# Another hand-annealed order table for a fused attention and feed-forward kernel

## The chip, the core and the metric

The kernel runs on one core of one Trainium2 chip. A core has a matrix engine (TensorE, PE in the profile), a vector engine (VectorE, DVE), a scalar engine (ScalarE, ACT), a general engine (GpSimd, POOL) and a sync engine (SyncE, SP) that here only issues DMAs. Each engine has a queue of its own that it works through strictly in order, and the engines meet through semaphores. The metric is the device time of one execution in microseconds. The kernel before took 668.05 us, the median of three runs from 667.8 to 668.63.

## What is computed

One transformer layer with 2048 tokens of width 640, attention with 32 query heads of width 20 that share one key head and one value head, and beside it a feed-forward block of width 1536 with a squared ReLU. Both read the same normalised input, and both results are added to the input:

```python
xn = _layernorm(x, axis=-1)
return x + _A_ref(xn, A_wq, A_wk, A_wv, A_wo) + _B_ref(xn, B_w1, B_b1, B_w2, B_b2)
# _A_ref: scores = q k^T * Dh**-0.5; p = softmax(scores); o = p v; out = o wo
# _B_ref: h = relu(x w1 + b1)**2; out = h w2 + b2
```

The scores are 32 x 2048 x 2048 numbers, and each has to go through an exponential.

## The kernel before

**Tiles and stages.** A block is four heads by 512 queries, and there are 32 blocks. Within a block the 2048 keys are cut into 16 key tiles of 128. A score tile is one head, 128 keys and 512 queries: one matmul with 20 rows of contraction into one of the seven free banks of PSUM, and there are 2048 of them. The matmuls of up to four heads sit in four row strips of the matrix engine and run side by side; the text calls such a set of score matmuls a **burst**. Everything else on the matrix engine runs in four column strips of 32: the sums of probabilities times values, the projections, the feed-forward layers and the output. Changing between row strips and column strips is a change of mode.

**Two ways to the exponential.** 696 instructions on ScalarE take two score tiles each (L1274, tile PT). The other 656 tiles make 164 **sets** of four: VectorE turns each tile into 16-bit integers that, read as bf16, are an exponential with a straight line between powers of two (L1497). Three more copies of the set with shifted integers are made by **passes**, either on GpSimd (an INT64_ADD, L1517) or on VectorE (L1518, with both listed at L1517 and L1518 as the alternatives `POOL` and `DVE`). The four copies are terms of one better exponential. They are summed by the matrix engine in that each term is multiplied with the values and accumulated (tiles x_sb or tmore with vx or vxs). Two terms of equal weight can instead be added first: by a DMA with accumulation that GpSimd issues (L1534), called a **pair sum**, or by VectorE (L1539, or L1913 where it was chosen afterwards). Then the matrix engine has one group of four matmuls less. The accumulators of a block are all in one bank.

**Who sets the order.** A greedy planner inside the kernel (L1648 and after) first makes a list of instructions for each engine. Then the table `PLAN` (L414) replaces these lists: for each engine it holds, entry by entry, how far down the list of instructions not yet taken the next one stands. A zero takes the next one. The key `on` has one digit for each of 820 choices (five for each of 164 sets): for three passes whether GpSimd (0) or VectorE (1) makes them, and for two pairs whether the matrix engine takes both terms (0), a DMA adds them (1) or VectorE adds them (2). The key `held` names, for instructions of GpSimd, the instruction of VectorE that they have to wait for, so that the two don't use the shared access to memory at the same time.

**The replay.** The function `replay` (L298) walks the five ordered lists once while the program is built, with a duration for each instruction and a latency for each dependence (the inner function `reach`, L307). On the chip the order on each engine is that of the table. What replay decides is which bank of PSUM a score tile or an accumulation takes (the one that it holds to be free first), the order in which waits are worked out, and which first and last matmul of a block opens and closes the sum. The same rules were used outside the kernel to anneal the table.

Of the kernel before, what the change touches and what calls it, by code (L numbers as in the profile page):

```python
# [79 lines left out]
ADM = 0.7  # L80
ADMP = 0.7
ADLEAD = 1.24
# [89 lines left out]
STOP = None  # L172
# [122 lines left out]
RC = dict(SAME=0.0027, CR=0.105, RC=0.098, FIRST=0.010, LANE=0.004, ACT=0.9035, ACTPE=0.2215, POOLP=1.008, AD=0.915, QK=0.425, DVEPE=0.155, STOP=114, STOPT=1.2)  # L295


def replay(seq, pool, order_all):  # L298
    ptr = {e: 0 for e in seq}
    free = {e: 0.0 for e in seq}  # L300
    start, fin, land = {}, {}, {}
    order_all.clear()
    mode, lock, dma, nadd, lastlock = "C", 0.0, 0.0, 0, None
    lane = [0.0] * HPG
    held = {}

    def reach(d, o):  # L307
        if d.dma is not None:
            return land[d] + ((ADMP if o.eng == "PE" else ADM) if d.add and not o.add else 0.0)
        if o.add and d.eng == "POOL":  # L310
            return fin[d] + ADPL + 0.035
        if d.eng == "PE":
            if o.eng == "PE":
                return start[d]
            return start[d] + (RC["QK"] if d.mode == "R" else d.dur + 0.2005) + (0.0 if o.eng == "ACT" else 0.02)
        if d.eng == "ACT" and o.eng == "PE":
            return fin[d] + (RC["ACTPE"] if d.name[:3] == "ACT" else LATS["ACT", "PE"])
        if d.eng == "DVE" and o.eng == "PE":
            return fin[d] + RC["DVEPE"]
        return fin[d] + LATS.get((d.eng, o.eng), 0.1)  # L320

    while True:
        best = None
        for e, ops in seq.items():
            if ptr[e] >= len(ops):
                continue
            o = ops[ptr[e]]
# [8 lines left out]
            for d in o.deps:  # L336
                t = max(t, reach(d, o))
            if o.lock:
                t = max(t, lock)
                if e == "POOL" and lastlock is not None:  # L340
                    t = max(t, fin[lastlock] + LATS["DVE", "POOL"])
# [32 lines left out]
        if e == "PE":  # L374
            if o.mode == "R":
                held["t"], held["o"] = t, o
                for h in o.lanes:
                    lane[h] = t + 0.2133 + RC["SAME"]
# [1707 lines left out]
```

## Time and profile before

| what | value |
|---|---|
| median of three runs | 668.05 us |
| the profiled execution | 669.29 us |
| its span from first to last instruction | 667.5 us |
| granted clock of the matrix engine | 1.000 |
| ScalarE exponentials (L1274) | 696, 641.1 us busy |
| score matmuls | 2048 |
| DMA pair sums (L1534) | 122 |
| DMA traffic | 100.51 MB |

The profiled execution is 1.24 us longer than the median, and 1.8 us of it lie around the span. The profile is one execution. Its page gives busy times for each engine, groups of instructions with mean duration, and the chain of work that ended last. Matmuls overlap in the pipeline, so a matmul's listed duration is longer than the time from one start to the next, and a busy matrix engine can still be waiting a little. All matmuls of the column strips and of the scores come from one helper, line L675, so they are told apart by tile names: `ps<-qT,kT` is a score matmul.

### The profile page before, as it was taken

The numbers are of one execution on the slowest core, as the hardware profiler recorded it, in microseconds if no ns is written. First come the engines' busy times: TensorE is split into PE (matmuls) and PEld (weight loads), VectorE is DVE, ScalarE is ACT, GpSimd is POOL, SyncE is SP. The second block draws the span as 40 slices with busy tenths as digits, with TensorE's granted clock in tenths as the row PEclk, the third lists the DMA queues.
The fourth block names the chain that finished last, engine by engine and source line by source line (L and its number), as shares of the span: only waits on it lengthen the run. The fifth ranks groups of instructions, "written<-read, shape, count | busy, mean of one in ns | idle before, by whom it ended". The sixth has DMA issues, their size and how long they took to land.

```text
span 667.5 us, 22412 instructions
## 1 busy us (share of the span) xinstructions
PE 659.2 (99%) x9618; PEld 213.7 (32%) x9618; DVE 623.0 (93%) x1120; ACT 650.2 (97%) x719; POOL 538.9 (81%) x549
## 2 busy tenths in 40 slices
PE   8999999999999999999999999999999999999998
PEld 4532222332322223333332222233233322223345
DVE  8879999899899999999999999999999999999997
ACT  7999999999999999999999999999999999999995
POOL 1608899998998898898888999988889999888600
DMA  8893756888768997777868577677688776438642
GB/s 290 233 249 76 149 98 145 162 178 169 144 147 167 182 178 145 153 152 154 165 133 165 112 156 145 134 155 136 145 166 172 138 144 137 96 63 165 142 108 76
DMA packets 53208, 100.51 MB, mean 151 GB/s; under 512 B 15980, under 2 KB 31228, under 8 KB 53044
## 3 DMA queue, kind: packets, MB, share of 16 engines
q0 software_dynamic: 18224, 66.59, 53.7%
q1 hardware_dynamic: 34308, 32.11, 16.8%
q8 instruction: 75, 1.23, 0.8%
q10 hardware_dynamic: 576, 0.38, 0.2%
q14 instruction: 25, 0.20, 0.1%
HBM read 23.26 MB, written 10.01 MB: 50 GB/s over the span
## 4 chain that ended last, share of the span: by engine, by line
PE 89%; DMA 6%; POOL 3%; DVE 1%; issue 0%; ACT 0%
PE ps L675 88%; DMA x_sb<-tmore 3%; POOL tmore L1517 1%; DMA x_sb<-x_sb 1%; DMA tmore<-tmore 1%; POOL x_sb L1517 1%; PE ps L880 1%; PE ps L851 0%; POOL tmore L1534 0%; PE ps L910 0%; PE ps L812 0%; DVE tmore L1497 0%; DVE OR L752 0%; ACT PT L1274 0%; DVE ident L689 0%
## 5 line engine op out<-in xcount | busy, mean ns | idle before, releaser
L1274 ACT ACTIVATE PT<-ps 128x1024 bf16<-128x1024 f32 x696 | 641.1, 1114 | 5.8 <-PE ps L675 5.2
L1497 DVE TENSOR_SCALAR tmore<-ps 128x512 uint16<-128x512 f32 x656 | 424.8, 683 | 25.2 <-PE ps L675 16.3
L675 PE MATMUL ps<-qT,kT 20*128 20x512 bf16 x2048 | 265.0, 384 | 0.5 <-ACT PT L1274 0.5
L1517 POOL INT64_ADD tmore<-tmore x200 | 216.0, 1119 | 36.4 <-DVE big L1008 17.4
L1517 POOL INT64_ADD x_sb<-tmore x202 | 219.7, 1117 | 20.0 <-DVE big L1008 6.2
L675 PEld LDWEIGHTS ps<-qT,kT 20*128 20x128 bf16 x2048 | 68.2, 91 | 253.4 <-issue 75.7
L675 PE MATMUL ps<-PT,vx 128*32 128x512 bf16 x1392 | 130.0, 384 | 0.0
L675 PE MATMUL ps<-w_sb,big 128*32 128x320 bf16 x1536 | 80.0, 302 | 0.0
L675 PE MATMUL ps<-xnT,w_sb 128*32 128x512 bf16 x960 | 77.7, 383 | 0.0
L1534 POOL DMA_DIRECT2D tmore<-tmore x63 | 63.3, 1004 | 9.1 <-DVE tmore L1518 4.7
L675 PE MATMUL ps<-x_sb,vxs 128*32 128x512 bf16 x624 | 59.5, 383 | 1.0 <-DMA x_sb<-x_sb 1.0
L675 PE MATMUL ps<-tmore,vxs 128*32 128x512 bf16 x632 | 60.4, 383 | 0.0
L1534 POOL DMA_DIRECT2D x_sb<-tmore x54 | 52.4, 970 | 5.3 <-POOL x_sb L1517 3.0
L675 PE MATMUL ps<-tmore,vx 128*32 128x512 bf16 x528 | 50.8, 384 | 0.6 <-DMA tmore<-tmore 0.6
L675 PEld LDWEIGHTS ps<-PT,vx 128*32 128x32 bf16 x1392 | 33.5, 94 | 39.5 <-issue 34.0
L675 PEld LDWEIGHTS ps<-w_sb,big 128*32 128x32 bf16 x1536 | 33.1, 95 | 30.6 <-issue 22.0
L1000 DVE TENSOR_SCALAR hT_tmp<-ps,b1col 128x512 bf16<-128x512 f32 x48 | 35.7, 743 | 2.9 <-PE ps L675 2.4
L1518 DVE TENSOR_SCALAR tmore<-tmore 128x2048 uint16<-128x2048 uint16 x47 | 32.8, 708 | 1.4 <-PE ps L675 1.3
L675 PE MATMUL ps<-x_sb,vx 128*32 128x512 bf16 x328 | 32.0, 384 | 1.1 <-DMA x_sb<-tmore 1.1
L675 PE MATMUL ps<-xnT,wq_sb 128*32 128x512 bf16 (+2 forms) x480 | 33.0, 356 | 0.0
L675 PE MATMUL ps<-wo_c,OC 128*32 128x320 bf16 x576 | 31.1, 301 | 0.0
L1518 DVE TENSOR_SCALAR x_sb<-tmore 128x2048 uint16<-128x2048 uint16 x43 | 29.4, 692 | 0.0
(100 smaller groups left out, 320.4 us busy)
## 6 DMA issues: line engine op xcount, KB each, us to landing
tmore<-tmore POOLq DMA_DIRECT2D x63, 512.0 KB, 5.7
x_sb<-tmore POOLq DMA_DIRECT2D x54, 512.0 KB, 5.7
w_sb<-in_B_w_dram SPq DMA_DIRECT2D x8, 480.0 KB, 10.7
big<-OR SPq DMA_DIRECT2D x71, 40.0 KB
xb<-in_A_x_dram SPq DMA_DIRECT2D x1, 2560.0 KB, 12.1
xb<-b2r POOLq DMA_DIRECT2D x1, 2560.0 KB, 19.3
xr<-xb SPq DMA_DIRECT2D x16, 160.0 KB, 4.3
out_dram<-out_sb SPq DMA_DIRECT2D x15, 160.0 KB, 3.6
```

Of the source, the lines that this page charges most:

```text
L675: return lambda e: e.matmul(out_(), l, r, start=val(start), stop=val(stop), tile_position=tp, skip_group_check=loose)
L880: return [(lambda e, dt=dt: e.transpose(out=psbf(bk)[:, dt * 128:(dt + 1) * 128], in_=xn_sb[:, st, dt:D:DT], identity=ident[:])) for dt in ...
L1000: o = Op(f"RL{qc}_{f}", "DVE", 0.66, [lambda e: e.tensor_scalar(out=hT_tmp[:, k % 2, :], in0=ps[:, at(bk), :], scalar1=b1col[:, f:f + 1], ...
L1274: o = Op(f"ACT{st_['j']}", "ACT", ACB + ACM * n, [lambda e: e.activation(out=PT[:, s0:s0 + n, :], in_=src(), func=AF.Exp, bias=-EXP_SHIFT, ...
L1497: d1 = op(f"D1_{n}_{i}", "DVE", 0.60, lambda e: e.tensor_scalar(out=L[:, cs].bitcast(U16), in0=ps[:, ref.n, :], scalar1=XA, scalar2=XB, op ...
L1517: fns = dict(POOL=lambda e, T=T, j=j: e.int64_add(out=T.bitcast(I64), in0=L.bitcast(I64), in1=TSTEP * j * 0x0001000100010001), DVE=lambda ...
L1518: DVE=lambda e, T=T, j=j: e.tensor_scalar(out=T.bitcast(U16), in0=L.bitcast(U16), scalar1=TSTEP * j, scalar2=None, op0=ALU.add))
L1534: p = op(f"AD{a}_{n}", "POOL", ADDUR, lambda e, src=src, dst=dst: e.dma_start(dst, src, accum_op=ALU.add), dp + [ad_last.get(k)], dma=adse ...
```

## The change

Nothing of the computation changes, nor the greedy planner. Two things do. First, the replay gets other latencies. A pair sum reaches its consumer `ADLATE` = 0.6 us after its modelled landing, where the kernel before had 0.7 us for every engine. A score burst reaches ScalarE after 0.44 us and VectorE after 0.422 us, where it was 0.425 and 0.445 us. A burst of n tiles is 0.004 us longer for each tile after the first. VectorE to GpSimd takes 0.2 us, where it was 0.17, and 0.21 us more ahead of a pair sum. GpSimd sees the matrix engine 0.07 us later. Second, the whole table `PLAN` is another one: the order lists of all four engines PE, DVE, POOL and SP, `held` and `on`.

```diff
+ADLATE = 0.6
...
-RC = dict(SAME=0.0027, CR=0.105, RC=0.098, FIRST=0.010, LANE=0.004, ACT=0.9035, ACTPE=0.2215, POOLP=1.008, AD=0.915, QK=0.425, DVEPE=0.155, STOP=114, STOPT=1.2)
+RC = dict(SAME=0.0027, CR=0.105, RC=0.098, FIRST=0.010, LANE=0.004, ACT=0.9035, ACTPE=0.2215, POOLP=1.008, AD=0.915, QK=0.44, QKD=0.422, POOLIN=0.07, DVEAD=0.21, DVEPE=0.155, STOP=114, STOPT=1.2)
...
-            return land[d] + ((ADMP if o.eng == "PE" else ADM) if d.add and not o.add else 0.0)
+            return land[d] + (ADLATE if d.add and not o.add else 0.0)
...
-            return start[d] + (RC["QK"] if d.mode == "R" else d.dur + 0.2005) + (0.0 if o.eng == "ACT" else 0.02)
+            if d.mode == "R":
+                return start[d] + RC["QK" if o.eng == "ACT" else "QKD"]
+            return start[d] + d.dur + 0.2005 + (0.0 if o.eng == "ACT" else 0.02) + (RC["POOLIN"] if o.eng == "POOL" else 0.0)
...
+        if d.eng == "DVE" and o.eng == "POOL":
+            return fin[d] + 0.2 + (RC["DVEAD"] if o.add else 0.0)
...
-                    t = max(t, fin[lastlock] + LATS["DVE", "POOL"])
+                    t = max(t, fin[lastlock] + 0.2)
...
-                    lane[h] = t + 0.2133 + RC["SAME"]
+                    lane[h] = t + 0.2133 + RC["SAME"] + RC["LANE"] * (len(o.lanes) - 1)
```

Of the table, the digits and entries can be counted in the diff:

| count in `PLAN` | before | after |
|---|---|---|
| passes on GpSimd / on VectorE | 402 / 90 | 394 / 98 |
| pairs left to the matrix engine | 200 | 200 |
| pairs added by DMA | 122 | 120 |
| pairs added by VectorE | 6 | 8 |
| choices of 820 that differ | | 105 |
| leading entries that are the same (PE, DVE, POOL, SP) | | 178, 138, 26, 23 |

168 rows, old and new, of the table PLAN are left out of this document.

## The prediction

> **What bounds the kernel now.** I read the page first, for the engines and the chain that ended last.
>
> ```profile
> span 667.5 us, 22412 instructions
> PE 659.2 (99%) x9618; PEld 213.7 (32%) x9618; DVE 623.0 (93%) x1120; ACT 650.2 (97%) x719; POOL 538.9 (81%) x549
> PE 89%; DMA 6%; POOL 3%; DVE 1%; issue 0%; ACT 0%
> L1274 ACT ACTIVATE PT<-ps 128x1024 bf16<-128x1024 f32 x696 | 641.1, 1114 | 5.8 <-PE ps L675 5.2
> ```
>
> The matrix engine is listed as busy for 99% of the span and 89% of the chain is its own. ScalarE is second with 97%, VectorE third. What is left of the chain is 6% DMA and 3% GpSimd; where that comes from follows below. The busy times by stretches (PE, PEld, DVE, ACT, POOL; counts in brackets) say that this holds from one end to the other:
>
> ```profile
> 200.00:300.00 100.00, 100.00 (x1394) 29.85 (x1394) 96.00 (x164) 99.78 (x110) 90.91 (x92) 1.00 0.82 162
> 300.00:400.00 100.00, 99.02 (x1401) 29.61 (x1391) 95.19 (x162) 98.89 (x109) 88.46 (x89) 1.00 0.75 149
> 640.00:667.50 27.50, 24.69 (x539) 12.89 (x535) 22.44 (x38) 20.48 (x25) 0.00 (x0) 1.00 0.25 82
> ```
>
> So an order table can win in two places only: in gaps of the matrix engine, and in what its order itself costs. The second is seen in the timeline of the matrix engine, where I look at starts (first column), not at durations:
>
> ```profile
> 283.80 0.40 PE L675 MATMUL ps<-qT,kT 20*128 20x512 bf16 x4
> 284.12 0.40 PE L675 MATMUL ps<-tmore,vx 128*32 128x512 bf16 x4
> 284.35 0.39 PE L675 MATMUL ps<-PT,vx 128*32 128x512 bf16 x4
> 284.67 0.39 PE L675 MATMUL ps<-qT,kT 20*128 20x512 bf16 x3
> 284.99 0.40 PE L675 MATMUL ps<-x_sb,vx 128*32 128x512 bf16 x4
> ...
> 287.51 0.39 PE L675 MATMUL ps<-qT,kT 20*128 20x512 bf16 x2
> 287.83 0.40 PE L675 MATMUL ps<-xnT,wq_sb 128*32 128x512 bf16 x4
> ```
>
> A group of four column matmuls followed by another takes 284.35 - 284.12 = 0.23 us. Followed by a score burst it takes 284.67 - 284.35 = 0.32. The burst itself takes 0.32 until the next column group, with two, three or four tiles alike (287.51, 284.67, 283.80). So a burst costs 0.32 + 0.09 = 0.41 us whatever it carries, and two bursts made into one save 0.41.
>
> ```profile
> L675 PE MATMUL ps<-qT,kT x2048: 371/385/386, 11.8 to 656.3; 20*128 20x512 bf16 x187
> ```
>
> Between the first of these 2048 starts (11.8) and the last (656.3) I count 659 bursts, 3.1 tiles in each. They take 659 x 0.41 = 270 us of the span. 13 of them run a second wave of tiles at once behind the first; merging further is possible but rare now.
>
> The gaps are in the list of waits of PE:
>
> ```profile
> PE ps L675 <- DMA x_sb<-tmore: 1.1, 3, 0.5
> PE ps L675 <- DMA x_sb<-x_sb: 1.0, 1, 1.0
> PE ps L675 <- DMA tmore<-tmore: 0.6, 1, 0.6
> ```
>
> All are pair sums that land after the matrix engine wants them: five gaps, 2.7 us. Their place is in the chain of work (start, length), and the largest one in the timeline:
>
> ```profile
> 160.32 7.27 DMA tmore<-tmore
> ...
> 351.31 7.75 DMA x_sb<-x_sb
> ...
> 471.28 6.85 DMA x_sb<-tmore
> ...
> 542.95 7.63 DMA x_sb<-tmore
> ...
> 607.75 7.54 DMA x_sb<-tmore
> ```
> ```profile
> 357.73 0.40 PE L675 MATMUL ps<-tmore,vxs 128*32 128x512 bf16 x4
> 359.10 0.40 PE L675 MATMUL ps<-x_sb,vxs 128*32 128x512 bf16 x4 [0.97 <-DMA x_sb<-x_sb]
> 359.43 0.39 PE L675 MATMUL ps<-qT,kT 20*128 20x512 bf16 x3
> 359.85 0.69 DVE L1497 TENSOR_SCALAR tmore<-ps 128x512 uint16<-128x512 f32 x1 [0.73 <-PE ps L675]
> 359.89 1.02 ACT L1274 ACTIVATE PT<-ps 128x1024 bf16<-128x1024 f32 x1 [0.99 <-PE ps L675]
> ```
>
> From 357.73 to 359.10 are 1.37 us where 0.23 is normal, so 1.14 are lost though 0.97 are listed: the listed gap starts only at the end of the last matmul in the pipeline, 0.17 after the next could have started. Five such gaps lose 2.7 + 5 x 0.17 = 3.5 us. ScalarE and VectorE have nothing left either after this one (0.99 and 0.73 idle), so it is a loss of the whole kernel. That is 0.5% of the span, and the only sizeable gap in the middle of it.
>
> **The change part by part.** *The work of the matrix engine.* The table leaves 200 pairs to it as before, so no group of matmuls is added or removed: 0.
>
> *The work of VectorE and GpSimd.* Eight passes move from GpSimd to VectorE, pair sums by DMA fall by two, and additions on VectorE rise by two.
>
> ```profile
> L1517 POOL INT64_ADD tmore<-tmore x200 | 216.0, 1119 | 36.4 <-DVE big L1008 17.4
> L1534 POOL DMA_DIRECT2D tmore<-tmore x63 | 63.3, 1004 | 9.1 <-DVE tmore L1518 4.7
> L1518 DVE TENSOR_SCALAR tmore<-tmore 128x2048 uint16<-128x2048 uint16 x47 | 32.8, 708 | 1.4 <-PE ps L675 1.3
> L1913 DVE TENSOR_TENSOR tmore<-tmore 128x2048 bf16<-128x2048 bf16 x2 | 2.4, 1216 | 0.0
> L1497 DVE TENSOR_SCALAR tmore<-ps 128x512 uint16<-128x512 f32 x656 | 424.8, 683 | 25.2 <-PE ps L675 16.3
> ```
>
> By busy time, GpSimd loses 8 x 216.0/200 + 2 x 63.3/63 = 8.6 + 2.0 = 10.6 us. VectorE gains 8 x 32.8/47 + 2 x 2.4/2 = 5.6 + 2.4 = 8.0 us. Its load goes from 623 to 631 us; spread over the 600 us between start and end that is 1.3 us in each 100, and its fullest stretch (96.00) goes to 97.3. I cost it at nothing, because 25.2 us idle ahead of its score tiles cover it. Without that cover the score tiles come late by up to 8.0 us in all, and the bursts behind them find a bank fewer. In the other direction nothing is gained: GpSimd's 10.6 us are off the chain except just before a late sum. The ends are 0 and +8.0; I take 0, nearest to the idle row.
>
> GpSimd does wait behind such passes, by the list of its waits:
>
> ```profile
> POOL tmore L1517 <- DVE x_sb L1518: 6.8, 7, 1.6
> ```
>
> Seven times, 6.8 us, is 1 us each. If each of the ten instructions that VectorE gains does that, GpSimd loses about 10 of its 10.6 us again, and the sums that wait behind its passes start no earlier than now.
>
> The Trainium skill has a rule that speaks against this exchange (SBUF — State Buffer, section "Who interferes with whom"): a VectorE instruction in a two-port mode, or one with two inputs in SBUF, holds the port pair it shares with GpSimd for the whole instruction, and GpSimd blocks. By it 8.0 us, the busy time that VectorE gains, would be lost to GpSimd. The row agrees in direction, but no row here separates such a block from the waits that the order itself writes into `held`.
>
> *The pair sums.* The page has their median from issue to landing at 5.7 us; the five late ones took 6.9 to 7.8. The old replay brought a sum to its reader 1.24 + 4.36 + 0.7 = 6.3 us after its issue when no other was under way, the new one 6.2. So against the words of the change the sums land 0.1 us earlier in it. Its other numbers do fit the trace better: at 359.43 the burst reached VectorE in 0.42 us (new 0.422, old 0.445) and ScalarE in 0.46 (new 0.44, old 0.425), and a burst of three is 0.322 in it where the old had 0.314 and the rows show 0.32. The old plan thus ran up to 659 x 0.008 = 5.3 us ahead on the matrix engine, and readers of sums that it put at the last moment came early or late by chance. All five late sums can be gained (-3.5), or as many more be lost (+3.5, five more of the same mean size). I take half of the gain, -1.75: the replay's clock is better, its landing is not.
>
> *The order of the rest.* All four lists are new from entry 179 (PE), 139 (DVE), 27 (POOL) and 24 (SP); the start is thus as before. SyncE issues the same transfers in another order, to readers that in no row of PE's list of waits were kept by them, so 0; if one is, it costs about what one late sum does, 3.5 / 5 = 0.7 us. The number of bursts is not readable from the table. From above and below, I allow about as many as run in two waves now, 10 either way: 10 x 0.41 = 4.1 us. I take three fewer, -1.2 us, because an order planned with the right length of a burst has less reason to split one.
>
> **Sum.** -1.75 - 1.2 + 0 = -3.0 us. From the profiled execution that is 669.29 - 3.0 = 666.3. The median of the runs shown lies 1.24 below that execution, so the forecast is 668.05 - 3.0 = 665.0 us, 0.45% faster. Its own range is 661.5 to 666.7.
>
> **Rivals.** *The trades cancel* (within 0.2%, that is 1.3 us, about the least that measuring this kernel can tell from no change). The five late sums are replaced by as many others, and the bursts stay at 659 give or take three: 668.0, between 666.7 and 669.4. For it speaks that the work of PE is the same to the group and that its landing model is not better; against it that every list changes, so that an exact balance would be chance.
>
> *The sums land late* (slower). This is also the case in which the change does not do what it says. With 0.1 us less for each landing, and GpSimd held up at ten more places, more readers stand ahead of their sums. The price is 3.5 us for five more late ones: 671.5. It decides from the point where waits of PE on DMA go past 2.7 us in the list. For it speak the five rows of the chain, each led in by GpSimd's passes; against it that there are two sums fewer.
>
> *VectorE becomes the bound* (slower). If a third of its 8.0 us comes out as late score tiles, the time is 668.05 + 2.7 = 670.7. It decides where VectorE is idle for less than about 17 us ahead of L1497, 25.2 less 8.0, and the matrix engine waits in its place. For it speaks the stretch with 96.00 of 100; against it that VectorE itself waited 16.3 us for the matrix engine.
>
> **How the numbers follow.** The forecast has 0.53. The trades cancel: 0.19. Late sums 0.17, VectorE 0.11. So faster by over 0.2% has 0.53, within 0.2% 0.19, slower 0.28. The range goes from the forecast's lower end, 661.5 (both gains nearly in full: -3.5 and seven bursts), to 671.0, which holds the case of VectorE and about half of the late sums. I leave out about 1 in 10 on each side.
>
> **What would show it.** Right: waits of PE on DMA at 0.5 to 1.5 us, two or three late sums in the chain, 650 to 658 bursts, PE's busy time 2 to 4 us down, VectorE at 630 to 632. Wrong for the sums: five or more DMA pieces of over 6.8 us in the chain. Wrong for the bursts: 660 or more, or ones with fewer than 3.1 tiles. Wrong for VectorE: ScalarE waiting more than 5.2 us for PE while no DMA is named, and under 17 us idle ahead of L1497. A gain of more than 5 us would mean that bursts, not gaps, were what the table could still win.

## The result and the profile after

The changed kernel takes 667.37 us, the median of 20 runs (666.64 to 668.53). The kernel before took 668.63 on the same chip, also from 20 runs. The ratio is 0.9979, with a 95% interval of 0.9971 to 0.9987, so the change makes the kernel 0.21% faster. The forecast was 665.0, 0.45% faster. The direction was right, the size under half, and the range (661.5 to 671.0) holds the time.

The profiled execution took 667.37 us, against 669.29. Its page, the same lines as before:

```profile
span 665.5 us, 22453 instructions
PE 659.5 (99%) x9618; PEld 214.3 (32%) x9618; DVE 629.1 (95%) x1130; ACT 649.9 (98%) x719; POOL 530.1 (80%) x539
PE 74%; ACT 23%; DMA 1%; DVE 1%; POOL 0%; issue 0%
L1277 ACT ACTIVATE PT<-ps 128x1024 bf16<-128x1024 f32 x696 | 640.9, 1118 | 4.1 <-PE ps L678 3.5
L1500 DVE TENSOR_SCALAR tmore<-ps 128x512 uint16<-128x512 f32 x656 | 423.6, 683 | 20.2 <-PE ps L678 11.8
```

The span of the profiled execution is 2.0 us shorter. VectorE has 6.1 us more work and GpSimd 8.8 less. VectorE still idles 20.2 us ahead of its score tiles, above the 17 that the prediction set as the bound. PE's busy time has not fallen, though the span has. The new thing is in the third line: the chain that ended last ran 0% through ScalarE and 89% through PE before, and now 23% through ScalarE and 74% through PE. DMA fell from 6% to 1%, and the list of PE's waits says why:

```profile
PE ps L678 <- ACT PT L1277: 0.5, 1, 0.5
PE ps L678 <- DMA tmore<-tmore: 0.5, 1, 0.5
```

Before there were five waits on DMA with 2.7 us, now there is one with 0.5. The chain (start, length) has the one late sum and, right behind it, the stretches of ScalarE:

```profile
159.22 7.58 DMA tmore<-tmore
166.85 0.88 PE ps L678 x10
167.75 80.93 ACT PT L1277 x88
248.72 122.26 PE ps L678 x1801
```

In the third row 88 exponentials follow each other in 80.93 us, 0.92 us each, and the chain leaves ScalarE for no other engine on the way. The waits of PE's weight loads (total, times, longest) have moved the same way. First the kernel before, then the changed one:

```profile
PEld ps L675 <- DVE tmore L1497: 75.7, 198, 0.4
PEld ps L675 <- ACT PT L1274: 62.8, 167, 0.8
```
```profile
PEld ps L678 <- ACT PT L1277: 142.1, 371, 0.8
PEld ps L678 <- DVE tmore L1500: 48.9, 130, 0.4
```

A weight load that waits for an exponential waits for the bank that the exponential empties. Such waits went from 167 to 371, those for VectorE from 198 to 130. Most are hidden, since a weight load is ahead of its matmul. Neither the chain nor this list proves which engine sets the pace. In the experiments below the kernel before, with 0% of its chain on ScalarE and 167 such waits, gets hardly more than the changed one from less work for PE. And the changed kernel with shorter exponentials, 4.4 us faster, still lists 358 such waits while its chain has 0% of ScalarE. The end of the chain's ScalarE stretch shows a wait that is not hidden, in the timeline of the changed kernel (rows of PE and of its weight loads):

```profile
247.93 0.39 PE L678 MATMUL ps<-xnT,w_sb 128*32 128x512 bf16 x4
248.25 0.85 PE L678 MATMUL ps<-qT,kT 20*128 20x512 bf16 x5
249.04 0.40 PE L678 MATMUL ps<-xnT,wq_sb 128*32 128x512 bf16 x4
```
```profile
248.72 0.09 PEld L678 LDWEIGHTS ps<-qT,kT 20*128 20x128 bf16 x2 [0.37 <-ACT PT L1277]
```

This burst of five tiles takes 249.04 - 248.25 = 0.79 us. Five tiles need two waves in four row strips. In the burst at 440.83 us of the same trace the second wave starts 0.23 us after the first, here 248.72 - 248.25 = 0.47, so about 0.24 us of it are the wait for a bank. The prediction's burst, in one wave, took 0.32.

From the starts of all matmuls I counted three things in both traces. Column groups that follow one another (from 43 us on) take 214.7 us before and 212.1 after, so 2.6 less: these are the late sums, and one is left. There are 659 and 656 bursts, three fewer as forecast, worth 3 x 0.41 = 1.2 by the prediction's price. But the time inside bursts fell by only 0.35 us where 3 x 0.32 = 0.96 was due, and the time lost ahead of bursts rose by 1.35. So 2.0 us went into waits for banks, and -2.6 - 1.2 + 2.0 = -1.8 stands for the -2.0 of the span.

### The profile page after: what moved, and what is told of

Its sections match the earlier page's. It is cut to its first block, busy times and chain, and to the rows that moved or that the text cites. A ratio compares the mean times of both kernels' runs of the same rounds, so it can differ in the third digit from the quotient of the medians.

```text
span 665.5 us, 22453 instructions
## 1 busy us (share of the span) xinstructions
PE 659.5 (99%) x9618; PEld 214.3 (32%) x9618; DVE 629.1 (95%) x1130; ACT 649.9 (98%) x719; POOL 530.1 (80%) x539
## 4 chain that ended last, share of the span: by engine, by line
PE 74%; ACT 23%; DMA 1%; DVE 1%; POOL 0%; issue 0%
PE ps L678 72%; ACT PT L1277 23%; DMA tmore<-tmore 1%; PE ps L883 1%; PE ps L854 0%; POOL tmore L1520 0%; PE ps L913 0%; DVE tmore L1500 0%; PE ps L815 0%; POOL x_sb L1520 0%; DVE ident L692 0%; DVE PT L690 0%; DVE OR L755 0%; DVE OC L1401 0%; DVE tmore L1521 0%
## 5 line engine op out<-in xcount | busy, mean ns | idle before, releaser
L1500 DVE TENSOR_SCALAR tmore<-ps 128x512 uint16<-128x512 f32 x656 | 423.6, 683 | 20.2 <-PE ps L678 11.8
L1520 POOL INT64_ADD tmore<-tmore x196 | 211.6, 1109 | 34.3 <-DVE OR L1365 9.4
L1520 POOL INT64_ADD x_sb<-tmore x198 | 212.3, 1109 | 26.2 <-DVE tmore L1521 8.4
L1537 POOL DMA_DIRECT2D tmore<-tmore x60 | 58.4, 974 | 8.8 <-POOL tmore L1520 5.3
L1521 DVE TENSOR_SCALAR tmore<-tmore 128x2048 uint16<-128x2048 uint16 x51 | 35.5, 703 | 0.0
L1521 DVE TENSOR_SCALAR x_sb<-tmore 128x2048 uint16<-128x2048 uint16 x47 | 33.0, 707 | 0.0
```

The costliest lines, as they stand in the source:

```text
L1500: d1 = op(f"D1_{n}_{i}", "DVE", 0.60, lambda e: e.tensor_scalar(out=L[:, cs].bitcast(U16), in0=ps[:, ref.n, :], scalar1=XA, scalar2=XB, op ...
L1520: fns = dict(POOL=lambda e, T=T, j=j: e.int64_add(out=T.bitcast(I64), in0=L.bitcast(I64), in1=TSTEP * j * 0x0001000100010001), DVE=lambda ...
L1521: DVE=lambda e, T=T, j=j: e.tensor_scalar(out=T.bitcast(U16), in0=L.bitcast(U16), scalar1=TSTEP * j, scalar2=None, op0=ALU.add))
L1537: p = op(f"AD{a}_{n}", "POOL", ADDUR, lambda e, src=src, dst=dst: e.dma_start(dst, src, accum_op=ALU.add), dp + [ad_last.get(k)], dma=adse ...
```

## The experiments

A ratio is always to the kernel before, run on the same chip beside it. Theory one was that PE's gain is passed on only in part, because ScalarE and the banks that it frees set the pace. Theory two was the prediction's premise, that a microsecond of PE is a microsecond of the kernel. Theory three was that the banks that the replay picks make the difference, not the order.

**The changed kernel again.** The identical kernel, two more times, on two chips.

```diff
  (no edit: open the changed kernel once more)
```

> The changed kernel itself, unchanged, on the chip of these runs, to have it beside them: all theories 1.0 to 1.9 us faster than before.

> The changed kernel itself once more, beside the tuned order on the same chip: between 0 and 1.4 us faster than before, as in the two measurements so far.

Measured: 667.33 against 667.52, ratio 0.9998 (0.9989 to 1.0007), and 667.35 against 667.74, ratio 0.9993 (0.9985 to 1.0002). The changed kernel took 667.3 to 667.4 three times. It is the kernel before that ranges from 667.5 to 668.6. The mean of the three ratios is 0.9990, so the gain is nearer to 0.1% than to 0.2%, and in two of three pairs it can't be told from nothing. In the profiles of these two executions PE has no wait on DMA left at all.

**ScalarE cut short.** Every exponential after the first 16 leaves out 64 of 512 columns (448), in both kernels, or 6 of 512 (506), in the changed one. The output lacks those exponentials.

```diff
+            w = 512 if st_["j"] < 16 else 448
-                return ps[:, refs[0].n:refs[-1].n + 1:step, :]
+                return ps[:, refs[0].n:refs[-1].n + 1:step, 0:w]
-  ... e.activation(out=PT[:, s0:s0 + n, :], in_=src(), ...
+  ... e.activation(out=PT[:, s0:s0 + n, 0:w], in_=src(), ...
```

> The changed kernel with every exponential on ScalarE after the first 16 over 448 instead of 512 columns of each tile, which leaves 64 columns of each tile out; orders and banks as in the changed kernel. ScalarE has about 0.1 us less in each of 680 instructions. If it is the waits for banks that ScalarE frees that took the gain back, they go: 3 to 5 us faster than the changed kernel. If ScalarE were the bound of the whole, it would be 30 us or more. If the matrix engine alone is the bound and its waits are of other kinds, less than 1.5 us.

> The kernel before with ScalarE's exponentials after the first 16 over 448 of 512 columns, which leaves 64 columns of each tile out; order and banks as before. In the changed kernel this took 5.4 us off the profiled span, and nearly all waits inside and ahead of bursts went. If those waits are where the changed kernel gave its gain back (theory one), before has fewer of them to lose: 3 to 4 us faster than before, and the changed order then leads by about 4 us instead of 2. If they are no larger in the changed kernel, it is 5.4 us faster and the lead stays at 2.

> The changed kernel with ScalarE's exponentials after the first 16 over 506 of 512 columns, which leaves 6 columns of each tile out: 0.010 us less in each of 680 instructions (904 against 797 ns for 128 columns in the earlier cut), 6.8 us of ScalarE, about what was taken from the matrix engine before. If ScalarE sets the pace at the margin (theory one): 4 to 6.8 us faster than the changed kernel. If both engines set it together, so that a cut in one alone buys little: 1.5 us or less.

**PE cut short.** In every eighth set the groups that sum VectorE's terms, apart from a block's first and last, multiply 256 of 512 columns (64 groups of the kernel before, 68 of the changed one). The sums lack the other half. Last, this cut together with the 506.

```diff
+                    w = 256 if s["n"] % 8 == 0 and not ends[0] and not ends[1] else 512
-  ... ps[32 * h:32 * h + 32, PVB, :], wgt[:, kt, :], src[:, i * 512:(i + 1) * 512] ...
+  ... ps[32 * h:32 * h + 32, PVB, 0:w], wgt[:, kt, :], src[:, i * 512:i * 512 + w] ...
```

> The kernel before with 64 of the 528 groups that multiply terms with values over 256 instead of 512 queries, which leaves half of those terms out; order and banks as before. The matrix engine has 64 x 0.107 = 6.8 us less. Theory two: 6.8 us faster than before. Theory one: 3 to 5 us, since ScalarE's pace takes part of it back.

> The changed kernel with the same cut in 68 groups: the matrix engine has 68 x 0.107 = 7.3 us less. Theory two: 7.3 us faster than the changed kernel. Theory one: 2 to 4 us, less than in the kernel before, as more of its bursts start on ScalarE's release.

> Both cuts at once in the changed kernel: 6.8 us less for ScalarE and 7.3 us less for the matrix engine (leaving out 6 columns of each tile and half of 68 terms). If ScalarE sets the pace: at most 1 us more than its cut alone. If both set it together: 6 to 7 us faster than the changed kernel, though each cut alone gave under 1.5.

Measured:

| kernel | cut | time, before beside it | ratio (95%) | span |
|---|---|---|---|---|
| changed | ScalarE 448 | 661.62, 667.87 | 0.9899 (0.9886 to 0.9912) | 660.1 |
| before | ScalarE 448 | 664.26, 667.52 | 0.9949 (0.9937 to 0.9962) | 661.8 |
| changed | ScalarE 506 | 662.90, 667.62 | 0.9932 (0.9919 to 0.9944) | 661.1 |
| before | PE, 64 groups | 667.03, 667.52 | 0.9992 (0.9983 to 1.0001) | 666.3 |
| changed | PE, 68 groups | 667.14, 667.52 | 0.9992 (0.9983 to 1.0001) | 665.5 |
| changed | both | 661.97, 667.62 | 0.9911 (0.9897 to 0.9924) | 660.3 |

The cuts of PE and of ScalarE by nearly the same time decide it. The page of the PE cut, and one halved group in its timeline:

```profile
span 665.5 us, 22452 instructions
PE 658.3 (99%) x9617; PEld 216.8 (33%) x9618; DVE 628.7 (94%) x1130; ACT 649.7 (98%) x719; POOL 530.0 (80%) x539
```
```profile
202.51 0.29 PE L1316 MATMUL ps<-tmore,vx 128*32 128x256 bf16 x4
202.65 0.61 PE L678 MATMUL ps<-xnT,w_sb 128*32 128x512 bf16 x8
```

This group takes 202.65 - 202.51 = 0.14 us (0.12 is the commonest) where 0.23 is normal. By the starts the 68 groups save 6.4 us, and the span is the changed kernel's to the tenth. All of it comes back around the bursts: 4.1 us inside them and 2.7 ahead of them. PE stays at 99% because a matmul is listed until its modelled end, well after the next could start, so that short waits leave no gap. Now the cut of ScalarE to 506 columns:

```profile
span 661.1 us, 22452 instructions
L1278 ACT ACTIVATE PT<-ps x696: 1008/1058/1184, 12.2 to 651.3; 128x1012 bf16<-128x1012 f32 x170, 128x1024 bf16<-128x1024 f32 x4
```

The commonest step from one exponential to the next fell from 904 to 894 ns. 680 steps of 10 ns are 6.8 us less for ScalarE, and the span fell by 4.4. The waits at bursts fell by 4.7 in my count, with PE's work unchanged. So at this margin a microsecond of ScalarE is worth 0.65 us of the kernel, and one of PE about 0.03 (0.2 of 6.4, by the times beside the repeat on the same chip). In the kernel before, 6.4 us less for PE bought 0.5 (0.08 each), so the premise was wrong there too, though the cut to 506 was not run in it. Theory two falls. Theory one holds in kind but not in size: it expected 3 to 5 and 2 to 4 us from the two cuts of PE, and nearly all came back. With both cuts the span is 660.3, 0.8 less than with ScalarE's alone: the PE cut then bought something, yet still only an eighth of itself.

The cut to 448 columns lets the shortest steps go down to 797 ns, so it could take off 680 x (904 - 797) ns = 73 us. It gives 5.4 us of span, 1.0 more than 6.8 us did. Then ScalarE waits for PE, by its list (the changed kernel, then the cut one):

```profile
ACT PT L1277 <- PE ps L678: 3.5, 11, 0.9
```
```profile
ACT PT L1278 <- PE ps L678: 22.9, 91, 1.1
```

So by these runs ScalarE stands only about 5 us above what PE allows, and once it is relieved by that much it meets PE. That the changed order leads by more once ScalarE is out of the way (1.7 by the spans, 3.3 by the ratios, from two chips) stays unclear.

**The pair sums made short.** Each DMA adds 1024 of 2048 columns, with nothing moved in order. The other half of each sum is left out.

```diff
-  ... e.dma_start(dst, src, accum_op=ALU.add)
+  ... e.dma_start(dst[:, 0:1024], src[:, 0:1024], accum_op=ALU.add)
```

> The kernel before with every pair sum over 1024 of its 2048 columns, which leaves half of each sum out; order and banks as before. The sums land earlier, so no reader is late, and nothing is moved. In the profile of before ScalarE's next step came 0.4 to 1.1 us late after each of five late sums. If these are what the change won, this is 2.0 to 3.5 us faster than before. If a late sum is mostly handed back at the next steps, it is under 1 us.

> The changed kernel with the same cut of its pair sums. One late sum is left to win: 0.6 us faster than the changed kernel. If late sums are what the change won, it has no lead over the kernel before with the same cut, or is behind it; if the change won elsewhere, it leads by 1 to 2 us here too.

Measured: before with half sums 666.31 against 667.62, ratio 0.9978 (0.9969 to 0.9987), and the changed kernel with half sums 666.76, ratio 0.9987 (0.9979 to 0.9996). The DMA list (count, size, median us to landing) and the span, first of the kernel before:

```profile
tmore<-tmore POOLq DMA_DIRECT2D x63, 512.0 KB, 5.7
```
```profile
span 664.4 us, 22411 instructions
...
tmore<-tmore POOLq DMA_DIRECT2D x63, 256.0 KB, 3.7
```

The sums land 2 us earlier, no wait of PE on DMA is left, and the span falls by 3.0 us. Set side by side by the nth exponential, the two traces part in five steps at the five late sums (0.78, 1.10, 0.35, 0.57 and 0.45, together 3.25). That is the 3.5 of the prediction, one sum after the other. The waits at bursts stayed the same within 0.1 us: here PE's gain reached the span whole. Behind a late sum VectorE or ScalarE had stood still as well. By the medians the cut was worth 1.3, under the 2.0 to 3.5 that were expected, and in the changed kernel 0.6 (667.35 from other chips, 666.76). With all sums in time the order of before is 0.45 us ahead of the changed order, from one chip. So the change's gain in the profile is the late sums, and no gain shows from the rest of its order.

**Readers of late sums moved.** Six readers of sums go 2 to 4 column groups later in the table of before, two readers later in the changed one, and eight readers earlier in the changed one. The last two runs repeat the moves with every bank held as it was (`pin`), since a move makes the replay choose other banks: 250 of 1482 choices in the kernel before, 5 in the changed one, 552 for the earlier readers.

```diff
+        for name, n in (('DPV6_10_1', 4), ('DPV26_12_1', 3), ('DPV16_12_2', 4), ...):
+            pe = seq["PE"]
...
+            pe.remove(o)
+            pe.insert(j, o)
```
```diff
+  if o.name in PIN:
+      if any(bk not in can for bk in PIN[o.name]): continue
+      can = {bk: can[bk] for bk in PIN[o.name]}
```

> The table of before, with six readers of pair sums moved two to four column groups later in the matrix engine's list; everything else as before. In the trace of before these six lost 0.71, 0.69, 1.14, 0.45, 0.16 and 0.39 us, 3.5 in all. Theory one (the matrix engine's gain is passed on in part, since bursts then wait for banks that ScalarE frees): 1.5 to 2.5 us faster than before. Theory two (a microsecond taken from the matrix engine is a microsecond of the kernel): 3.5 us faster. Theory three (it is the choice of banks by the replay that makes the difference, not the sums): within 0.7 us of before.

> The changed kernel with the one late reader (0.64 us lost) and the next one at its limit moved four and one column groups later. Theory one: 0.3 us faster than the changed kernel, theory two: 0.6 us, theory three: nothing.

> The changed kernel with eight readers of pair sums moved earlier, to 0.5 to 0.95 us before the landing that the trace shows, 5.9 us in all. Theory one: 3 to 4 us slower than the changed kernel. Theory two: 5.9 us slower. Theory three: within 0.7 us of the changed kernel.

> The same six readers of pair sums moved later in the table of before, but each score tile and accumulation keeps the bank of PSUM that it had in the kernel before. If the loss of the earlier try came from the 250 other banks (theory three) and a late sum costs what it shows on the matrix engine (theory two), this is 2.5 to 3.5 us faster than before. If a late sum's time is mostly handed back at the next wait for ScalarE (theory one), it is 0.5 to 2 us faster. If moving the readers itself did the harm, it is slower again by 3 to 4 us.

> The changed kernel with the late reader and the next one at its limit moved later and all banks kept. Theories two and three: 0.5 us faster than the changed kernel, and so the fastest so far by a little; theory one: 0.3 us faster.

Measured: 1.0065 (1.0046 to 1.0084), 0.9996 (0.9988 to 1.0005) and 1.0164 (1.0142 to 1.0185) without pins. With pins 1.0011 (1.0002 to 1.0021) for the kernel before and 1.0005 (0.9996 to 1.0013) for the changed one.

The first was expected to gain and lost 4.2 us. At three of the four late sums from 350 us on it gained 0.45 to 1.1 each, but it lost 4.0 between 153 and 175 us, in a stretch whose banks had changed. Not all of that is banks. The largest piece, 1.5 us, is one group of PE that waits for a pass of GpSimd, which stands behind another pass that waited for VectorE:

```profile
157.61 1.04 POOL L1517 INT64_ADD x_sb<-tmore  x1 [1.24 <-DVE OC L1398]
```
```profile
160.97 0.40 PE L675 MATMUL ps<-x_sb,vxs 128*32 128x512 bf16 x4 [1.40 <-POOL x_sb L1517]
```

The replay also decides for which instruction of VectorE such a pass waits. In this program the pass at 157.61 waits for one (tile OC) for which it doesn't wait in the kernel before or in the pinned one. Pinned, the kernel gains at all six places, 3.7 us by steps, and gives 3.3 back behind them: at 154, 168 and 615 us more than the gain, at 479 half, at 360 0.4 of 1.1, at 551 nothing. Its span is 667.3, 0.2 less than before; by the medians it is 0.1% slower. One place that gives all back is at 615 us. The kernel before, with the reader ahead of the score tile:

```profile
615.33 0.40 PE L675 MATMUL ps<-x_sb,vx 128*32 128x512 bf16 x4 [0.38 <-DMA x_sb<-tmore]
...
615.41 0.69 DVE L1497 TENSOR_SCALAR tmore<-ps 128x512 uint16<-128x512 f32 x1 [0.61 <-DMA x_sb<-tmore]
```

And the pinned kernel, with the reader later:

```profile
615.04 0.69 DVE L1607 TENSOR_SCALAR tmore<-ps 128x512 uint16<-128x512 f32 x1 [0.64 <-DMA x_sb<-tmore]
...
615.79 0.39 PE L785 MATMUL ps<-qT,kT 20*128 20x512 bf16 x1 [0.36 <-DVE tmore L1607]
```

VectorE waits for the same landing in both, because its tile goes into the buffer that the sum read. Moving the reader frees PE, but the burst that it starts at 615.04 gets its last tile only at 615.79, in the bank that VectorE had not emptied. At 360 and 551 us, where most of the gain stays, no wait of VectorE on the landing is listed. The changed kernel's one late sum has another follower: pinned, 0.59 us are gained at 167 us and 0.79 lost at 169, where VectorE's copy of the finished block waits 0.91 us for PE, which runs the moved group late. Neither moving nor pinning gained anything over the changed kernel (667.8 and 668.2, after 667.35 on other chips). So a later reader helped only where nothing else waited, while a sum that lands earlier helped at every place.

The other direction is one-sided. The eight readers moved earlier cost 10.6 us of span (676.1 after 665.5). By PE's waits:

```profile
PE ps L678 <- DMA x_sb<-tmore: 2.7, 3, 1.9
PE ps L678 <- DMA tmore<-tmore: 2.2, 3, 0.9
PE ps L678 <- DMA tmore<-x_sb: 0.5, 1, 0.5
```

5.4 us are listed. The ScalarE steps at the eight places add up to 7.9, and another 3.2 are lost between 227 and 243 us, where the next pair of runs loses as much without a late sum. No theory had expected that much, the dearest 5.9.

**The latencies alone.** The changed table with the old latencies of the replay, and the table of before with the new ones. The order on every engine stays; 384 of 1482 banks differ in the first, 61 in the second. In the first, seven passes of GpSimd between 219 and 238 us also wait for another instruction of VectorE; in the second, only banks and the waits that come with them differ.

```diff
-RC = dict(... QK=0.44, QKD=0.422, POOLIN=0.07, DVEAD=0.21 ...)
+RC = dict(... QK=0.425 ...)
-            return land[d] + (ADLATE if d.add and not o.add else 0.0)
+            return land[d] + ((ADMP if o.eng == "PE" else ADM) if d.add and not o.add else 0.0)
```

> The new table with the old latencies in the replay: the order on each engine is that of the changed kernel, but 384 of 1482 places in PSUM are other banks. Theories one and two: within 0.5 us of the changed kernel. Theory three (the new latencies choose better banks): 1 us or more slower than it, back to the kernel before.

> The table of before with the new latencies in the replay: same order, 61 of 1482 banks differ. Theory three: as the order of before was annealed on the old latencies, its banks fit those, and others cost 1 to 3 us: slower than before. If the new latencies choose banks that are better on the chip whatever the table, it is faster by about 1 us. Theories one and two: within 0.5 us of before.

Measured: 1.0043 (1.0026 to 1.0061) for the new table with old latencies, span 669.3, and 1.0017 (1.0007 to 1.0027) for the old table with new ones, span 667.7. So the table and the latencies that it was made with belong together, and either half of the change alone is slower than no change. The first loses 3.3 of its 3.7 us between 227 and 243 us. PE there, in the changed kernel:

```profile
226.96 0.39 PE L678 MATMUL ps<-qT,kT 20*128 20x512 bf16 x3
227.28 0.40 PE L678 MATMUL ps<-PT,vx 128*32 128x512 bf16 x4
227.64 0.39 PE L678 MATMUL ps<-qT,kT 20*128 20x512 bf16 x2
```

And with the old latencies:

```profile
227.35 0.39 PE L673 MATMUL ps<-qT,kT 20*128 20x512 bf16 x2
228.03 0.38 PE L673 MATMUL ps<-qT,kT 20*128 20x512 bf16 x1 [0.29 <-ACT PT L1272]
228.34 0.40 PE L673 MATMUL ps<-PT,vx 128*32 128x512 bf16 x4
228.94 0.39 PE L673 MATMUL ps<-qT,kT 20*128 20x512 bf16 x2 [0.20 <-ACT PT L1272]
```

The same three tiles take 227.28 - 226.96 = 0.32 us in one wave, and 228.34 - 227.35 = 0.99 in two, since the third was given a bank that ScalarE still had to empty. In the changed kernel it takes one that VectorE had emptied. All waits of PE between 218 and 245 us name ScalarE, four with 1.1 us, and none names GpSimd or a sum. So banks are the likely cause of the whole stretch, but the seven other waits of GpSimd lie in it too and no run parts the two. The second run is the clean one: 61 other banks alone cost 0.17%, 1.4 us by the medians. Theory three is right as an effect of its own, of the size of the whole change.

**Another order, found on the replay.** A search over the changed table with the landing of sums set to 1.4 us moved 547 entries of PE, 162 of VectorE and 83 of GpSimd.

```diff
-ADLATE = 0.6
+ADLATE = 1.4
+        for e in TUNE:
+            old = seq[e]
+            seq[e] = [old[k] for k in unpack(TUNE[e], len(old))]
```

> The changed kernel with 547 of 3212 places in the matrix engine's list, 162 in VectorE's and 83 in GpSimd's changed by a search that used the kernel's own replay with a pair sum reaching its reader 1.4 us after its modelled landing instead of 0.6. Nothing is left out. In the profile of the changed kernel ScalarE loses 9.4 us in 45 steps that start over 0.06 us late. If it is these steps that can be won (theory one), and the later landing keeps readers off the sums, it is 1 to 2 us faster than the changed kernel. If orders found on the replay carry nothing to the chip beyond the late sums: within 0.6 us of it.

Measured: 667.02 against 667.74, ratio 0.9989 (0.9980 to 0.9998). The changed kernel itself, on the same chip, had 667.35, ratio 0.9993. The two can't be told apart, and no version here that computes everything is clearly faster than the changed kernel.

## Why the prediction was right and wrong

**What bounds the kernel.** "So an order table can win in two places only: in gaps of the matrix engine, and in what its order itself costs." The premise behind it, that PE's 99% makes it the bound, is the step that failed. In the changed kernel 6.4 us less work for PE changed the span by 0.0, and 6.8 us less for ScalarE by 4.4. In the kernel before 6.4 us less for PE bought 0.5. A busy share of 99% hides waits: a matmul is listed for 0.39 us where the next could start after 0.23, so one that waits 0.1 us for a bank leaves no gap. The prediction's own row for 200 to 300 us has ScalarE at 99.78 of 100 beside PE's 100.00, and between its first and last exponential (12.19 to 657.66 us) ScalarE is listed as busy for 639.9 of 645.5 us, PE for 641.6. Its 97% of the span is that low because the span has ends without exponentials.

**The pair sums (-1.75).** Right in place and, in the profile, more than right: of five late sums one is left. Column groups give 2.6 us. The half sums confirm the price of the five, 3.25 us by steps against 3.5 forecast. But the forecast took a price read in one execution, of 669.29, off a median of 668.05. By the medians the five are worth 1.3 and the one left 0.6, so by them the change won about 0.7 here: the term was more than twice too large. The sums seem to be late by less in most executions than in the profiled one. The kernel before's table with the new latencies lists 1.8 us of waits on DMA, with PE's cut 2.0, where the profile shown before had 2.7. The rival in which the sums land late did not come.

**Three fewer bursts (-1.2).** The count came to the unit, 656. That is luck: the prediction called the number not readable from the table, and no run tests its reason. That "two bursts made into one save 0.41" failed as a saving of the kernel. The bursts are 0.41 us of PE, and PE's time was not what was short: 2.0 us of waits for banks stand where the 1.2 should be, costed at nothing. This is the term of the sum that was missing.

**VectorE and GpSimd (0).** Right. VectorE gained 6.1 us instead of 8.0, to 629.1 where 630 to 632 was forecast, with 20.2 us still idle ahead of its score tiles. VectorE did not become the bound. GpSimd's 8.8 us showed no gain, as forecast. No run here parts the blocking of GpSimd that the prediction cited from the waits of the order.

**PE's busy time 2 to 4 us down.** Wrong, it is 659.5 after 659.2. It was no usable sign, for the same reason as the first point.

**The baseline.** The forecast used the median of three runs, 668.05. The kernel before measured 667.5 to 668.6 over its later groups of runs, a spread of 1.1 us where the forecast gain was 3.0 and the gain beside it 1.3. The rival in which the trades cancel (668.0, between 666.7 and 669.4) describes the time better than the forecast: 667.4 is 0.6 from it and 2.4 from 665.0. Its mechanism didn't come, though: the five late sums were not replaced by others. What cancelled in part were the waits at bursts. (The lower end of the forecast's own range, -3.5 and seven bursts, adds up to 661.7, not 661.5.)

**What stays open.** Why the kernel before differs between its groups of runs, on several chips, by up to 1.1 us while the changed one agrees to 0.1. Fewer late sums would do it, since their lateness varies, but no run was made for that. How much PE alone would allow without any bank waits was not measured either, nor how banks and GpSimd's waits share the loss of the new table with the old latencies.

## What to carry to other kernels

When several engines are busy for 93% or more, the page need not say which one sets the pace; here it named the wrong one. Take the same few microseconds from each in turn, with the order unchanged, and see which shortens the span. A plan that is worked out ahead for fixed resources is only as good as the latencies it was made with: its order and its latencies change together. The same order with 384 other banks and seven other waits of GpSimd lost more (2.7 us) than the whole change had won (1.3). When a plan is worked out again, compare all that it decides before one part is given the blame. Before moving a reader away from a late producer, look for who else waits for the same landing.

## What the runs showed of the hardware

The lines view of the changed kernel lists the exponentials with 1017 to 1269 ns (minimum, median, maximum, then first and last start in us):

```profile
L1277 ACT ACTIVATE PT<-ps x696: 1017/1124/1269, 12.2 to 655.8; 128x1024 bf16<-128x1024 f32 x174
```

Yet the next one commonly starts 904 ns after it. At 506 of 512 columns this is 894, so 10 / 12 = 0.83 ns for each column of an instruction's two tiles. At 448 the shortest steps are 797 ns, which fits the same price (107 / 128 = 0.84), though most are longer since ScalarE then waits for tiles.

A group of four column matmuls with half the columns takes 0.12 us instead of 0.23 when another column group follows, and about 0.22 instead of 0.32 when a burst does. The change of mode adds the same 0.1 us to both.

A pair sum's landing falls from 5.7 to 3.7 us when its bytes are halved, so, if the rest goes with the bytes, an estimate is that about 1.7 of the 5.7 do not depend on them (2 x 3.7 - 5.7).

The first 20 us differ between executions of the same kernel (busy PE, PEld, DVE, ACT, POOL; granted clock; DMA share, GB/s). The changed kernel in its first profile, and again on another chip:

```profile
0.00:20.00 20.00, 18.10 (x317) 9.39 (x321) 17.96 (x70) 15.19 (x28) 4.43 (x12) 1.00 0.89 292
```
```profile
0.00:20.00 20.00, 17.00 (x289) 8.84 (x290) 16.15 (x63) 13.44 (x26) 3.40 (x10) 0.91 0.89 307
```

The second has a granted clock of 0.91 there and two instructions of ScalarE fewer (26 after 28), and its span is 667.0 us instead of 665.5. It took 668.85 us, while the median of its runs is the same as the first's to 0.1 us. A single profile's span is thus no measure of 1 us of change; the spans in this text are to be read with that in mind, and the steps at one place count for more.
